# Nine weight transfers in place of six, and a new written order, in a linear-attention and mixer kernel

## The chip, the cores and the metric

The kernel runs on one core of a Trainium2 chip. The metric is device time in microseconds (us): the median of several runs of the whole kernel. Beside these runs stands one profiled execution, from which all durations of single instructions come. The engines have short names in the profile: PE is TensorE (matmuls; PEld its weight loads), DVE is VectorE, ACT is ScalarE, POOL is GpSimd and SP is SyncE, which here only issues transfers. DMA stands for the 16 engines that move data between the main memory (HBM) and the on-chip memory (SBUF). PSUM is the small memory into which PE writes.

## The reference

Inputs r, k and v have the shape (4, 8, 768, 48): four batches, eight heads, 768 steps, 48 channels. The first half is a linear attention with a decaying state for each head, the second half an MLP mixer over its result.

```python
for t in range(S):
    kt, vt, rt = (k[:, :, t], v[:, :, t], r[:, :, t])
    cur = np.einsum('bhd,bhe->bhde', u[None] * kt, vt)
    y[:, :, t] = np.einsum('bhd,bhde->bhe', rt, state + cur)
    state = w[None, :, :, None] * state + np.einsum('bhd,bhe->bhde', kt, vt)
...
xt = x.transpose(0, 2, 1)
h = np.maximum(xt @ w_tok1, 0.0) @ w_tok2
u = x + h.transpose(0, 2, 1)
h2 = np.maximum(u @ w_ch1, 0.0) @ w_ch2
return (u + h2).astype(np.float32)
```

Here x is y with the heads side by side, (4, 768, 384). The token weights are 768 x 256 and 256 x 768, the up weight w_ch1 is 384 x 1536 and the down weight w_ch2 is 1536 x 384.

## The kernel before, in words

**Units.** The attention is done in 24 units: four batches of six chunks of 128 steps (unit u is chunk u % 6 of batch u // 6). A unit loads k, r and v (three transfers of 192 KB, issued by SP). It scales k and r by powers of the decay (kp and rp, L658 and L661; each may run on POOL or DVE, both write the tile kpr), and casts v (vb, ACT). Units 0 to 13 transpose kp and rp on PE (trk, trr into the PSUM tile tr_ps) and copy them back by ACT, either as one copy (rk, L696) or in two halves (rkk and rkr, L700, for the units in `rk_two`); units 14 to 23 transpose by DMA (L684). PE then forms the scores (at, two PSUM tiles), which a causal mask turns into AT0 and AT1 on DVE (L727). For the units in `raw`, AT1 goes another way: ACT copies the scores to SBUF as bf16 (raw, L736), and DVE masks that copy (ATr, L740). PE multiplies with v (y) and with the state of the chunks before (yS), updates the state (kv on PE, S on DVE or ACT), and DVE adds the term of the current step (yd, on DVE or POOL) while it writes the unit's rows of x (L824, tile x_b).

**Mixer.** Once a batch's six units are done: hid (L831) multiplies x with w_tok1 into two PSUM tiles (h_ps), hr applies the relu, and w_tok2 brings it back to tokens. For the first half of batch 0 this is done directly in the transposed layout (ux, ub, uTm, L876 to L892, which write uT); the other halves go by bk, us, tu and uT (tiles hT_ps, u_sb, t_ps). Then z (L899) multiplies uT with w_ch1 in 12 column groups j of 128 for each group sg of three chunks (three matmuls each, 72 for a batch), zr applies the relu (ACT or DVE), and h (L910) multiplies with w_ch2, three column groups at a time (q = 0 to 3). os adds u and a transfer stores the result.

**Order.** Nothing of the order is written by hand. The class `Plan` (L45) holds a list of steps, each with the engines it may use and their assumed times, what it must come after, whether it takes one of four PSUM banks, and a rank. `run` (L72) plays time forward and always starts the open step with the lowest rank whose engine is free; attention has its unit's number as rank, the token half of batch b's mixer (hid to uT) about 6 b + 6.5, its z and h about 1000 + b, so that z and h fill what attention leaves. `graph` (L168) builds the steps, and the instructions are issued on each engine in the order of the plan. An engine's own instructions always run in that order; the semaphores between engines are set by the tile framework from what reads and writes what.

**Weights.** POOL issues the weight transfers (L645), because these convert from float32 to bf16 on the way. There are six: w_tok1, w_tok2, w_ch1 in two halves of 768 columns, and w_ch2 in two halves of rows. `wafter` in the table `CFG` (L436) gives each a step after which it is put into POOL's queue. In the trace they are the transfers to the tiles wtok (two) and wch (four). The load of k of unit 6 is held until the y of unit 5 (`hold`, L456). `fill` puts a few idle matmuls into PE's gaps ahead of the first z.

Of the kernel before, what the change touches and what calls it, by code (L numbers as in the profile page):

```python
# [24 lines left out]
C = S // T  # L25
# [9 lines left out]
class Step:  # L35
    def __init__(self, name, ways, after, take, give, rank, emit):
        self.name, self.ways, self.take, self.give, self.rank, self.emit = name, ways, take, give, rank, emit
        self.after = [a for a in after if a is not None]
        self.then, self.left, self.ready = [], len(self.after), 0.0
        self.engine = self.start = self.end = self.seen = self.sends = None  # L40
        for a in self.after:
            a.then.append(self)


class Plan:  # L45
# [26 lines left out]
    def run(self):  # L72
# [5 lines left out]
        while todo:  # L78
# [4 lines left out]
            while again:  # L83
                again = False
                for s in sorted(open_, key=lambda s: (s.rank, s.ready)):
                    if s.ready > now or (s.take and min(banks) > now):
                        continue
                    if s.sends is not None and len(sent) >= self.in_flight:
                        old = sent[-self.in_flight]
                        if old.seen is None or old.seen > now:  # L90
                            if old.seen is not None:
                                heapq.heappush(times, old.seen)
                            continue
                    way = min(s.ways, key=lambda w: max(now, free.get(w[0], 0.0)) + w[2] + (w[4] if len(w) > 4 else 0.0))
                    eng, busy, seen = way[:3]
# [72 lines left out]
def graph(do, cfg):  # L168
# [24 lines left out]

    loads, weights, fetched, gates, u_row = {}, {}, [], {}, None
    for n, (kind, i) in enumerate(cfg["transfers"]):
        if kind == "b":
            fetched.append(p.add("i:ub", [("SP", cfg.get("sp", 0.65), 0.65)], fetched[-1:], rank=-1000 + n, emit=do("ubc")))
            u_row = p.transfer("x:ub", fetched[-1], 0.63, 1.8, 0.0)
        elif kind != "w":
# [5 lines left out]
        else:  # L205
            weights[i] = n
    wx, wi = {}, {}

    def weight(i, after):
        wi[i] = s = p.add(f"i:w{i}", [("POOL", 0.9, cfg.get("wseen", 1.0), True)], after, rank=-50, emit=do("weight", i))  # L210
        took = cfg.get("wtime", (3.0, 2.6, 3.1, 7.7, 3.1) if 5 not in cfg["wafter"] else (3.0, 2.6, 3.1, 3.9, 3.1, 3.9))[i]
        wx[i] = p.transfer(f"x:w{i}", s, took, took + 1.0, -1.0)

    for i in cfg["wafter"]:
        weight(i, [])
    xs, S_prev, at_free, y_free, kv_read, yS_prev = {}, None, [], None, None, None
    kv_first, bank_read, scored = None, [], {}
    for u in range(NU):
# [19 lines left out]
        if u in turned:  # L238
            s = p.add(f"i:t{u}", [("SP", 1.35, 1.4)], [kp, rp], rank=-2000, emit=do("turn_unit", u))
            rk = p.transfer(f"x:t{u}", s, 1.56, 2.2, 0.0)  # L240
        else:
            trk = p.add(f"trk{u}", [("PE", 0.235 * f, 0.235 * f + 0.2)], [kp], take=True, rank=r, emit=do("trk", u))
            trr = p.add(f"trr{u}", [("PE", 0.235 * f, 0.235 * f + 0.2)], [rp, trk], rank=r - 0.5, emit=do("trr", u))
            if u == 0:
                p.wait(wu, [trr])
            if u in cfg.get("rk_two", ()):
                ways = [("ACT", 0.48, 0.65)] + ([("DVE", 0.38, 0.53, False, cfg["rk_dve"])] if "rk_dve" in cfg else [])
                rkk = p.add(f"rkk{u}", ways, [trk], rank=r, emit=do("rkk", u))
                rk = p.add(f"rkr{u}", ways, [trr], rank=r, emit=do("rkr", u))
            else:  # L250
                rkk = None
                rk = p.add(f"rk{u}", [("ACT", 0.909, 1.08)], [trr], rank=r, emit=do("rk", u))
            reads = [rk, rkk] if rkk else [rk]
            if u in by_pe:
                pr = p.add(f"pr{u}", [("DVE", cfg.get("prt", 0.5), 0.65)], [rk], rank=r - 0.3, emit=do("pr", u))
                reads.append(pr)
            p.add(f"trf{u}", [("-", 0.0, 0.0)], reads, give=[f"trk{u}"], rank=-5000)
# [64 lines left out]
    for b in range(B):  # L322
# [4 lines left out]
        early = old + [xs[b * C + c] for c in range(4)]  # L327
        bank = [p.add(f"hid{b}_bank{i}", [("PE", 0.0, 0.0)], early + [wx[0]], take=True, rank=r) for i in range(2)]
        for c in range(C):
            h = p.add(f"hid{b}_{c}", [("PE", 2 * MM * f, 2 * MM * f + 0.13)], [xs[b * C + c], h] + bank, rank=r, emit=do("hid", b, c))  # L330
        some_direct = [sg for sg in range(2) if (b, sg) in direct]
# [11 lines left out]
        for sg in range(2):  # L343
            if (b, sg) in direct:
                last = C * (b + 1) - 1
                for mm in range(3):
# [10 lines left out]
            for c in range(sg * G, sg * G + G):  # L357
                n = 3 if (b, c) in cfg.get("xpe", ()) else 2
                bk = p.add(f"bk{b}_{c}", [("PE", n * MM + 0.01 * (b > 0), n * MM + 0.13 + 0.01 * (b > 0))], hr + [wx[1]], take=True, rank=r + 0.01 * c, emit=do("bk", b, c))
                us = p.add(f"us{b}_{c}", [ACT1, DVEP] if n == 3 else [DVEP], [bk], give=[f"bk{b}_{c}"], rank=r, emit=do("us", b, c))  # L360
# [9 lines left out]
        for sg in range(2):  # L370
            zr = []
            for j in range(NJ):
                old = downs[2 * b + sg - 3] if 2 * b + sg >= 3 else []
                z = p.add(f"z{b}_{sg}_{j}", [("PE", 3 * MM, 3 * MM + 0.13)], old + uT[3 * sg:3 * sg + 3] + [wx[2] if j < NJ // 2 else wx[4]], take=True, rank=m + 0.1 * sg + 0.001 * j, emit=do("z", b, sg, j))
                ways = [ACT1, DVEP + (False, 0.3)] if b in cfg.get("zr_dve", range(B)) else [ACT1]
                zr.append(p.add(f"zr{b}_{sg}_{j}", ways, [z], give=[f"z{b}_{sg}_{j}"], rank=o, emit=do("zr", b, sg, j)))
            downs.append([])
            for si in range(3):
# [3 lines left out]
                for part in range(parts):  # L382
                    h, n, mm = None, f"{b}_{c}" + "ab"[part] * (parts > 1), MM / parts + (0.005 if parts > 1 else 0.0)
                    for q in range(4):
                        x = 3 * mm + (own if q == 0 else 0.0)
                        h = p.add(f"h{n}_{q}", [("PE", x, x + 0.13)], zr[3 * q:3 * q + 3] + [wx[3] if q < 2 else wx.get(5, wx[3]), h], take=(q == 0), rank=m + 0.1 * sg + 0.05 + 0.01 * si + 0.001 * part - (0.02 if q else 0), emit=do("h", b, c, q, part, parts))
                    ways = [ACT1, DVEP] if (b, sg) in direct else [DVEP]
# [8 lines left out]
    last = None  # L396
    for i, name in cfg["wafter"].items():
        p.wait(wi[i], [last] + [next(s for s in p.steps if s.name == name)])
        last = wi[i]
    for s in p.steps:  # L400
# [32 lines left out]
    + [('b', 0)]  # L433
    + [("u", u) for u in range(14, 24)]
    + [('w', 0), ('w', 1), ('w', 2), ('w', 4), ('w', 3), ('w', 5)],
# [30 lines left out]
def kernel(  # L466
# [529 lines left out]
```

## Time and profile before

| what | us |
| --- | --- |
| median of 3 runs | 165.49 |
| lowest and highest run | 165.25, 165.77 |
| span of the profiled execution | 166.5 |
| mean granted clock of PE in it | 0.990 |
| DVE, ACT and POOL busy in it | 106.8, 87.2, 65.3 |
| first z matmul starts | 30.92 |
| first matmul of the last batch's z after attention is over | 139.72 |
| last h matmul ends | 163.2 |

Times in the profile count from the first instruction of the span. The profiled execution's span is 1.0 us over the median of the timed runs. A group line of the profile gives engine, operation, the tile written and the tiles read, the shape, the count, then the busy time of all in us and the mean of one in ns, then the idle time of the engine just ahead of them and what ended it. A timeline line gives the start in us, the length, engine, operation, tiles and count, and in brackets the idle time before it. The line L512 is that of a helper that records each operation, so the tiles tell the steps apart.

### The profile page before, as it was taken

The numbers are of one execution on the slowest core, as the hardware profiler recorded it, in microseconds if no ns is written. First come the engines' busy times: TensorE is split into PE (matmuls) and PEld (weight loads), VectorE is DVE, ScalarE is ACT, GpSimd is POOL, SyncE is SP. The second block draws the span as 40 slices with busy tenths as digits, with TensorE's granted clock in tenths as the row PEclk, the third lists the DMA queues.
The fourth block names the chain that finished last, engine by engine and source line by source line (L and its number), as shares of the span: only waits on it lengthen the run. The fifth ranks groups of instructions, "written<-read, shape, count | busy, mean of one in ns | idle before, by whom it ended". The sixth has DMA issues, their size and how long they took to land.

```text
span 166.5 us, 3791 instructions
## 1 busy us (share of the span) xinstructions
PE 156.8 (94%) x1462; PEld 100.6 (60%) x1464; DVE 106.8 (64%) x219; ACT 87.2 (52%) x182; POOL 65.3 (39%) x80
## 2 busy tenths in 40 slices
PE   6797999599999999999999999999999999999991
PEld 1377764356677666666666665666656655665671
DVE  5189996300459989899989889977885582021031
ACT  3996743279198636579804452069154502904900
POOL 7839970000009647386785857103840000000000
PEclk9999999789999999999999999999999999999999
DMA  5999999999699899999999994999990028012012
GB/s 100 215 213 210 159 187 176 188 184 168 131 208 287 158 192 216 217 230 182 198 192 169 230 158 106 188 235 222 171 240 6 4 50 218 16 51 94 0 47 94
DMA packets 97427, 26.26 MB, mean 158 GB/s; under 512 B 90753, under 2 KB 97410, under 8 KB 97410
## 3 DMA queue, kind: packets, MB, share of 16 engines
q1 hardware_dynamic: 93920, 22.88, 67.2%
q0 software_dynamic: 3488, 3.15, 12.3%
q8 instruction: 11, 0.18, 0.5%
q14 instruction: 6, 0.05, 0.1%
q10 hardware_dynamic: 2, 0.00, 0.0%
HBM read 20.65 MB, written 4.72 MB: 152 GB/s over the span
## 4 chain that ended last, share of the span: by engine, by line
PE 79%; DMA 8%; POOL 5%; ACT 3%; issue 2%; DVE 1%; SPq 1%; POOLq 0%
PE h_ps L512 31%; PE z_ps L512 29%; DMA wch<-in_moe_w_ch_dram 6%; PE y_ps L512 4%; PE at_ps L512 4%; PE hT_ps L512 3%; PE tr_ps L512 3%; POOL kpr L512 3%; PE kv_ps L512 2%; DMA ld_v<-in_v_dram 2%; PE t_ps L512 1%; ACT rk L512 1%; POOL wtok L512 1%; SPq L512 1%; POOL yd L512 0%
## 5 line engine op out<-in xcount | busy, mean ns | idle before, releaser
L512 ACT ACTIVATE zr<-z_ps 128x384 bf16<-128x384 f32 x94 | 45.5, 492 | 47.5 <-PE z_ps L512 47.3
L512 PE MATMUL z_ps<-uT,wch 128*128 128x384 bf16 x288 | 53.6, 331 | 2.0 <-DMA wch<-in_moe_w_ch_dram 2.0
L512 PE MATMUL h_ps<-wch,zr 128*128 128x384 bf16 (+1 forms) x300 | 52.5, 319 | 0.0
L512 PEld LDWEIGHTS <-wch 128*128 128x128 bf16 x288 | 27.0, 99 | 18.8 <-DMA wch<-in_moe_w_ch_dram 2.4
L512 PEld LDWEIGHTS <-zr 128*128 128x128 bf16 x300 | 27.9, 98 | 15.5 <-issue 0.2
L512 POOL TENSOR_TENSOR yd<-vb,adg 128x384 f32<-128x384 bf16 x18 | 15.5, 860 | 46.5 <-ACT adg L512 27.9
L512 DVE TENSOR_TENSOR AT<-at_ps,mask 128x512 bf16<-128x512 f32 x43 | 27.9, 682 | 0.7 <-PE at_ps L512 0.6
L512 DVE TENSOR_TENSOR osb<-u_sb,h_ps 128x384 f32<-128x384 bf16 (+1 forms) x22 | 11.7, 533 | 23.4 <-PE h_ps L512 23.3
L512 POOL TENSOR_TENSOR kpr<-ld_r,wp 128x384 bf16<-128x384 f32 x16 | 16.6, 1036 | 5.3 <-ACT wp L512 2.8
L512 ACT COPY rk<-tr_ps 128x512 bf16<-128x512 bf16 (+1 forms) x20 | 15.0, 756 | 4.9 <-PE tr_ps L512 4.5
L512 PEld LDWEIGHTS <-kpr 128*128 128x128 bf16 x192 | 13.7, 107 | 6.0 <-POOL kpr L512 2.6
L512 DVE TENSOR_TENSOR x_b<-y_ps,yd 128x384 bf16<-128x384 f32 x24 | 13.2, 552 | 5.2 <-PE y_ps L512 5.1
L512 POOL TENSOR_TENSOR kpr<-ld_k,wn 128x384 bf16<-128x384 f32 x15 | 15.2, 1011 | 1.8 <-DMA ld_r<-in_r_dram 0.7
L512 PEld LDWEIGHTS <-rk 48*128 48x128 bf16 (+1 forms) x272 | 11.0, 99 | 6.4 <-issue 2.7
L512 ACT CAST vb<-ld_v 128x384 bf16<-128x384 f32 x24 | 12.3, 511 | 4.3 <-POOL kpr L512 3.1
L512 PE MATMUL tr_ps<-ident,kpr 128*128 128x128 bf16 x112 | 12.1, 245 | 2.4 <-ACT rk L512 1.4
L512 DVE TENSOR_TENSOR S<-kv_ps,bm 128x384 bf16<-128x384 f32 x13 | 7.2, 551 | 6.0 <-PE kv_ps L512 5.8
L512 DVE TENSOR_TENSOR u_sb<-x_b,hT_ps 128x384 bf16<-128x384 bf16 x21 | 10.4, 546 | 0.9 <-PE hT_ps L512 0.9
L512 PEld LDWEIGHTS <-wtok 128*128 128x128 bf16 x90 | 8.0, 98 | 4.8 <-issue 0.6
L512 PEld LDWEIGHTS <-AT 128*128 128x128 bf16 x192 | 8.4, 98 | 3.4 <-DVE AT L512 0.8
L512 PE MATMUL at_ps<-rk 48*128 48x128 bf16 x192 | 10.2, 229 | 0.2 <-ACT rk L512 0.2
L512 PE MATMUL h_ps<-x_b,wtok 128*128 128x384 bf16 x48 | 10.2, 326 | 0.0
(81 smaller groups left out, 145.4 us busy)
## 6 DMA issues: line engine op xcount, KB each, us to landing
ld_k<-in_k_dram SPq DMA_DIRECT2D x24, 192.0 KB, 3.8
ld_r<-in_r_dram SPq DMA_DIRECT2D x24, 192.0 KB, 3.8
ld_v<-in_v_dram SPq DMA_DIRECT2D x24, 192.0 KB, 3.8
out_dram<-osb SPq DMA_DIRECT2D x23, 192.0 KB, 2.6
wch<-in_moe_w_ch_dram POOLq DMA_DIRECT2D x4, 576.0 KB, 14.2
wtok<-in_moe_w_tok_dram POOLq DMA_DIRECT2D x2, 384.0 KB, 6.4
u_bc<-in_u_dram SPq DMA_DIRECT2D x1, 192.0 KB, 5.0
out_dram<-osb SPq DMA_DIRECT2D x2, 96.0 KB, 1.6
```

The costliest lines, as they stand in the source:

```text
L512: ins = tc.keep_in_program_order(f(*args, **kw))
```

## The change

It changes six things.

- The six weight transfers become nine: w_tok1 in two halves of rows, w_tok2 in two halves of columns, w_ch1 in two quarters (column groups 0 to 2 and 3 to 5) and one half, w_ch2 in two halves of rows as before. Each piece has its columns or rows, an assumed time, and the step after which POOL issues it. The first quarter of w_ch1 is issued ahead of the second half of w_tok2.
- Each step that uses a weight now waits in the plan for the pieces it reads alone (`got`).
- `raw` has ten units in place of five: 0, 1, 4, 5, 6, 7, 12, 13, 18, 19 (8 and 11 are no longer in it). `rk_two` has 1, 3, 4, 5, 6, 8 in place of 0, 1, 2, 3, 4, 6.
- A table `rank` shifts the ranks of 122 steps, by up to about 990 either way, and a table `on` pins 76 steps to one engine. Among these are kp0, rp0, rp1, kp2 and S0, S3 on DVE.
- Some assumed times differ (`pe_times`, `prt`, `slack`, the time of a transfer); they act on the order alone.
- `run` skips steps whose only engine is busy before it sorts them, and computes the fullness of the banks once. This does not alter which step is taken.

```diff
+        self.open_on = ways[0][0] if len(ways) == 1 else None
...
-                for s in sorted(open_, key=lambda s: (s.rank, s.ready)):
-                    if s.ready > now or (s.take and min(banks) > now):
+                full = min(banks) > now
+                for s in sorted([s for s in open_ if s.ready <= now and (s.open_on is None or free.get(s.open_on, 0.0) <= now)], key=lambda s: (s.rank, s.ready)):
+                    if s.take and full:
                         continue
...
-    for i in cfg["wafter"]:
-        weight(i, [])
+    for i, (of, lo, hi, took, after) in enumerate(cfg["pieces"]):
+        wi[i] = s = p.add(f"i:w{i}", [("POOL", 0.85, cfg.get("wseen", 1.0), True)], rank=-50 + 0.01 * i, emit=do("weight", i))
+        wx[i] = p.transfer(f"x:w{i}", s, took, took + cfg.get("wland", 1.3), -1.0 + 0.001 * i)
+
+    def got(of, lo, hi):
+        return [wx[i] for i, (o, a, b, _, _) in enumerate(cfg["pieces"]) if o == of and a < hi and b > lo]
...
+        if s.name in cfg.get("on", {}):
+            s.ways = [w for w in s.ways if w[0] == cfg["on"][s.name]]
+            s.open_on = s.ways[0][0] if len(s.ways) == 1 else None
...
-    wafter={0: 'x:r4', 1: 'x:r4', 2: 'rp5', 4: 'kp5', 3: 'rp5', 5: 'rp5'},
-    slack={'v5': 3.0},
+    pieces=[
+        ('t1', 0, 3, 1.45, 'kp4'),
+        ('t1', 3, 6, 1.45, 'rp4'),
+        ('t2', 0, 3, 1.25, 'x:r5'),
+        ('c1', 0, 3, 1.9, 'x:r5'),
+        ('t2', 3, 6, 1.25, 'x:r5'),
+        ('c1', 3, 6, 1.9, 'x:k5'),
+        ('c1', 6, 12, 3.3, 'x:v5'),
+        ('c2', 0, 6, 4.0, 'rp5'),
+        ('c2', 6, 12, 4.0, 'rp4')],
+    slack={'v5': 1.6},
...
-    raw=(0, 1, 5, 8, 11),
-    rk_two=(0, 1, 2, 3, 4, 6),
+    raw=(0, 1, 4, 5, 6, 7, 12, 13, 18, 19),
+    rk_two=(1, 3, 4, 5, 6, 8),
...
-    pe_times=((0.33, 0.243, 0.185), (0.33, 0.243, 0.185)),
+    pe_times=((0.42, 0.21, 0.175), (0.42, 0.21, 0.175)),
...
-    late={'kp2': -0.6},
+    late={},
...
+    on={
+        'S0': 'DVE', 'S3': 'DVE', 'adg7': 'DVE', 'adg8': 'DVE', 'adg9': 'ACT', 'hr2_0': 'DVE', 'hr2_1': 'DVE',
+        'kp0': 'DVE', 'kp12': 'DVE', 'kp13': 'POOL', 'kp16': 'DVE', 'kp17': 'DVE', 'kp19': 'POOL', 'kp2': 'DVE',
+        'kp22': 'DVE', 'kp8': 'DVE', 'kp9': 'POOL', 'ku19': 'POOL', 'ku20': 'DVE', 'ku22': 'POOL', 'rku14': 'DVE',
+        'rku15': 'DVE', 'rku17': 'DVE', 'rku19': 'DVE', 'rp0': 'DVE', 'rp1': 'DVE', 'rp11': 'POOL', 'rp13': 'POOL',
+        'rp14': 'DVE', 'rp15': 'DVE', 'rp19': 'DVE', 'rp21': 'POOL', 'rp6': 'POOL', 'uT0_3': 'DVE', 'uT0_4': 'ACT',
+        'uT1_1': 'ACT', 'uT1_2': 'ACT', 'uT1_3': 'DVE', 'yd14': 'DVE', 'yd15': 'DVE', 'yd16': 'DVE', 'yd17': 'DVE',
+        'yd19': 'DVE', 'yd20': 'DVE', 'yd8': 'DVE', 'zr0_0_1': 'DVE', 'zr0_0_10': 'DVE', 'zr0_0_2': 'DVE',
...
+        'zr1_0_3': 'DVE', 'zr1_0_4': 'DVE', 'zr1_0_6': 'DVE', 'zr1_1_0': 'DVE', 'zr1_1_10': 'DVE', 'zr1_1_4': 'DVE',
...
     def weight(eng, i):
-        t, src = [(wtok1, moe_w_tok1), (wtok2, moe_w_tok2), (wch1, moe_w_ch1), (wch2, moe_w_ch2), (wch1, moe_w_ch1), (wch2, moe_w_ch2)][i]
-        cols = {2: slice(0, dch // 2), 4: slice(dch // 2, dch)}.get(i, slice(None))
-        rows = {3: slice(0, NJ // 2), 5: slice(NJ // 2, NJ)}.get(i, slice(None)) if 5 in CFG["wafter"] else slice(None)
+        of, lo, hi = CFG["pieces"][i][:3]
+        t, src = {"t1": (wtok1, moe_w_tok1), "t2": (wtok2, moe_w_tok2), "c1": (wch1, moe_w_ch1), "c2": (wch2, moe_w_ch2)}[of]
+        rows, cols = (slice(lo, hi), slice(None)) if of in ("t1", "c2") else (slice(None), slice(lo * 128, hi * 128))
         pool.dma_start(t[:, rows, cols], src.rearrange("(c p) k -> p c k", p=128)[:, rows, cols])
```

More of the change, by code (lines that the diff above doesn't have):

```diff
@@ L93, in run @@
                             continue
-                    way = min(s.ways, key=lambda w: max(now, free.get(w[0], 0.0)) + w[2] + (w[4] if len(w) > 4 else 0.0))
+                    way = s.ways[0] if len(s.ways) == 1 else min(
+                        s.ways, key=lambda w: max(now, free.get(w[0], 0.0)) + w[2] + (w[4] if len(w) > 4 else 0.0))
                     eng, busy, seen = way[:3]
@@ L192, in graph @@
     wgm = p.add("wGm", [("POOL", 1.1, 1.2, True), ("DVE", 0.47, 0.62, True)], [gd], rank=1.5, emit=do("wGm"))
-    loads, weights, fetched, gates, u_row = {}, {}, [], {}, None
+    loads, fetched, gates, u_row = {}, [], {}, None
     for n, (kind, i) in enumerate(cfg["transfers"]):
@@ L254, in graph @@
             if u in by_pe:
-                pr = p.add(f"pr{u}", [("DVE", cfg.get("prt", 0.5), 0.65)], [rk], rank=r - 0.3, emit=do("pr", u))
+                pr = p.add(f"pr{u}", [("DVE", cfg.get("prt", 0.36), 0.65)], [rk], rank=r - 0.3, emit=do("pr", u))
                 reads.append(pr)
@@ L327, in graph @@
         early = old + [xs[b * C + c] for c in range(4)]
-        bank = [p.add(f"hid{b}_bank{i}", [("PE", 0.0, 0.0)], early + [wx[0]], take=True, rank=r) for i in range(2)]
+        bank = [p.add(f"hid{b}_bank{i}", [("PE", 0.0, 0.0)], early + got("t1", 0, 1), take=True, rank=r) for i in range(2)]
         for c in range(C):
-            h = p.add(f"hid{b}_{c}", [("PE", 2 * MM * f, 2 * MM * f + 0.13)], [xs[b * C + c], h] + bank, rank=r, emit=do("hid", b, c))
+            h = p.add(f"hid{b}_{c}", [("PE", 2 * MM * f, 2 * MM * f + 0.13)], [xs[b * C + c], h] + bank + got("t1", c, c + 1), rank=r, emit=do("hid", b, c))
         some_direct = [sg for sg in range(2) if (b, sg) in direct]
@@ L358, in graph @@
                 n = 3 if (b, c) in cfg.get("xpe", ()) else 2
-                bk = p.add(f"bk{b}_{c}", [("PE", n * MM + 0.01 * (b > 0), n * MM + 0.13 + 0.01 * (b > 0))], hr + [wx[1]], take=True, rank=r + 0.01 * c, emit=do("bk", b, c))
+                bk = p.add(f"bk{b}_{c}", [("PE", n * MM + 0.01 * (b > 0), n * MM + 0.13 + 0.01 * (b > 0))], hr + got("t2", c, c + 1), take=True, rank=r + 0.01 * c, emit=do("bk", b, c))
                 us = p.add(f"us{b}_{c}", [ACT1, DVEP] if n == 3 else [DVEP], [bk], give=[f"bk{b}_{c}"], rank=r, emit=do("us", b, c))
@@ L385, in graph @@
                         x = 3 * mm + (own if q == 0 else 0.0)
-                        h = p.add(f"h{n}_{q}", [("PE", x, x + 0.13)], zr[3 * q:3 * q + 3] + [wx[3] if q < 2 else wx.get(5, wx[3]), h], take=(q == 0), rank=m + 0.1 * sg + 0.05 + 0.01 * si + 0.001 * part - (0.02 if q else 0), emit=do("h", b, c, q, part, parts))
+                        h = p.add(f"h{n}_{q}", [("PE", x, x + 0.13)], zr[3 * q:3 * q + 3] + got("c2", 3 * q, 3 * q + 3) + [h], take=(q == 0), rank=m + 0.1 * sg + 0.05 + 0.01 * si + 0.001 * part - (0.02 if q else 0), emit=do("h", b, c, q, part, parts))
                     ways = [ACT1, DVEP] if (b, sg) in direct else [DVEP]
@@ L396, in graph @@
     last = None
-    for i, name in cfg["wafter"].items():
-        p.wait(wi[i], [last] + [next(s for s in p.steps if s.name == name)])
+    for i, piece in enumerate(cfg["pieces"]):
+        p.wait(wi[i], [last] + [next(s for s in p.steps if s.name == piece[4])])
         last = wi[i]
@@ L433 @@
     + [('b', 0)]
-    + [("u", u) for u in range(14, 24)]
-    + [('w', 0), ('w', 1), ('w', 2), ('w', 4), ('w', 3), ('w', 5)],
-    wafter={0: 'x:r4', 1: 'x:r4', 2: 'rp5', 4: 'kp5', 3: 'rp5', 5: 'rp5'},
-    slack={'v5': 3.0},
+    + [("u", u) for u in range(14, 24)],
+    pieces=[
[9 more added lines that the diff above has]
+    slack={'v5': 1.6},
     pe_turn=(0, 1),
@@ L460 @@
     fill_from=16.5,
+    x_act=(),
+    rank={
[22 rows of a table added]
+    on={
[12 rows of a table added]
     fill=(0.24, 0.09, 0.13),
```

15 lines of the change are left out of this document (4 added, 11 removed), and 26 rows, old and new, of tables (on, rank).

## Prediction, made before the result was known

> **What bounds the kernel now.** I read the page first, for the share of each engine and the slices.
>
> ```profile
> span 166.5 us, 3791 instructions
> ...
> PE 156.8 (94%) x1462; PEld 100.6 (60%) x1464; DVE 106.8 (64%) x219; ACT 87.2 (52%) x182; POOL 65.3 (39%) x80
> ...
> PE   6797999599999999999999999999999999999991
> ```
>
> TensorE (PE) is full from the ninth slice (33 us) to the end; the holes lie ahead of it. So I cut the time into windows (columns: width, busy time and instructions of PE, PEld, DVE, ACT, POOL, then granted clock, DMA share, GB/s; in the second fence PE alone).
>
> ```profile
> 20.00:25.00 5.00, 4.67 (x73) 3.29 (x73) 5.00 (x12) 2.21 (x4) 4.11 (x5) 1.00 1.19 187
> ...
> 30.00:35.00 5.00, 4.08 (x21) 2.50 (x22) 0.72 (x2) 1.68 (x4) 0.00 (x0) 0.66 1.25 186
> ...
> 60.00:80.00 20.00, 19.49 (x237) 13.14 (x234) 18.39 (x38) 14.02 (x29) 12.64 (x14) 1.00 1.02 210
> ```
>
> ```profile
> 29.00:30.00 1.00, 0.00 (x0) 1.00 1.12 196
> ...
> 33.00:34.00 1.00, 1.00 (x5) 0.50 1.27 186
> ```
>
> Around 30 us PE stands still, and right after that it runs at half clock. Over 30 to 35 the granted clock is 0.66 on average, so 5 x 0.34 = 1.7 us of work is lost, in 3.4 us at 0.50. After that only 60 to 80 leaves idle time worth naming (0.5 us). PE's waits and the timeline name the cause.
>
> ```profile
> PE z_ps L512 <- DMA wch<-in_moe_w_ch_dram: 2.0, 1, 2.0
> ```
>
> ```profile
> 25.34 0.56 DVE L512 TENSOR_TENSOR x_b<-y_ps,yd 128x384 bf16<-128x384 f32 x1 [0.16 <-PE y_ps L512]
> ...
> 27.96 0.56 DVE L512 CAST uT<-ut_ps 128x384 bf16<-128x384 f32 x1 [0.76 <-PE ut_ps L512]
> 28.43 1.47 DVE L512 TENSOR_TENSOR u_sb<-x_b,hT_ps 128x384 bf16<-128x384 bf16 x3
> ...
> 30.92 0.85 PE L512 MATMUL z_ps<-uT,wch 128*128 128x384 bf16 x3 [2.02 <-DMA wch<-in_moe_w_ch_dram]
> ```
>
> Batch 0 of attention ends at 25.9 (x_b of unit 5). The transposed activations uT of the first group are ready at 28.5, but the first half of the up weight is there only at 30.9. The chain of waits (start, length, what) and POOL's queue say why.
>
> ```profile
> 20.86 10.02 DMA wch<-in_moe_w_ch_dram
> ...
> 31.77 1.05 PE t_ps L512 x9
> ...
> 111.79 3.42 PE z_ps L512 x21
> ```
>
> ```profile
> 18.15 0.78 POOL L512 DMA_DIRECT2D wtok<-in_moe_w_tok_dram  x1
> ...
> 20.86 3.26 POOL L512 DMA_DIRECT2D wch<-in_moe_w_ch_dram  x4
> ```
>
> The DMA engines are full (shares 1.19 and 1.25 above), and the weights pass in the order of issue. **The bound is DMA until 31 us, then PE.**
>
> **The change, part by part.** All sums are differences on the profiled execution, whose span of 166.5 is 1.0 over the median of 165.49; I take them off the median.
>
> *Nine pieces.* What lies ahead of the first up projection decides, so I need packet times. A packet is one row of one partition: 768 columns of 2 bytes make the large packets of 27.7 to 29.0 (wch1 alone on its queue, first row), 384 columns the small ones of 33 to 37 (wch2, second row).
>
> ```profile
> q0 software_dynamic: 173, 0.26, 110.7%
> ```
>
> ```profile
> q0 software_dynamic: 779, 0.59, 93.8%
> ```
>
> 1.107 x 16 x 1.3 us / 173 = 133 ns for a large packet; 0.938 x 16 x 4 / 779 = 77 ns for a small one. Before, wtok2 (256 large) and half of wch1 (384 large) take 640 x 133 / 16 = 5.3 us. After, half of wtok2 (256 small) and a quarter of wch1 (384 small) take 640 x 77 / 16 = 3.1 us. The first quarter lands at 30.9 - 2.2 = 28.7, against uT at 28.5: 1.8 of the 2.0 us go. If the slowest DMA engine is late whatever is queued, nothing goes (lower bound 0); the upper bound is the 2.0.
>
> The next quarter follows the other half of wtok2, 3.1 us later (31.8). Until then PE has three z of the first group and three of the second, 18 matmuls at 0.163 (3.42 / 21) = 2.9 us, and nine transposes (0.5 to 1.0; the row was at half clock): 3.4 or more for 3.1 us. But its order must wait for u_sb (29.9), so I charge 0.5 (bounds 0 and 1.5). The rest of wch1 needs 384 x 133 / 16 = 3.2 us more (35.0), under the next six z (2.9 us). With no gap of 2 us the clock stays up: 1.7 us gained (bounds 0 and 1.7).
>
> The row for the clock is the 0.50 above, right after a gap of 2.0 us. The Trainium skill, "TensorE: Matmul & The Clock Gate", section "HAM oscillation", sees the danger in idle gaps over about 3.4 us; by that rule this gap would have cost no clock, and the sum would lack the 1.7. The trace disagrees, so that outcome gets no chance of its own.
>
> Small packets cost DMA time: for wtok2 512 x 77 against 256 x 133, for half of wch1 768 x 77 against 384 x 133, together (39.4 - 34.0 + 59.1 - 51.1) / 16 = 0.8 us. Three more issues cost POOL 3 x 0.82 = 2.5 us (3.26 / 4 each); what queues behind them are kp and rp of unit 5. Their cover: kp0, rp0 and rp1 leave POOL (3 x 1.0 us, next rows).
>
> *Order and engines of batch 0.*
>
> ```profile
> L512 DVE TENSOR_TENSOR AT<-at_ps,mask 128x512 bf16<-128x512 f32 x43 | 27.9, 682 | 0.7 <-PE at_ps L512 0.6
> ...
> L512 POOL TENSOR_TENSOR kpr<-ld_k,wn 128x384 bf16<-128x384 f32 x15 | 15.2, 1011 | 1.8 <-DMA ld_r<-in_r_dram 0.7 <-PE z_ps L512 0.5 <-issue 0.5
> ...
> L512 DVE TENSOR_TENSOR kpr<-ld_r,wp 128x384 bf16<-128x384 f32 x8 | 4.7, 593 | 5.1 <-DMA ld_r<-in_r_dram 5.1
> ...
> L512 DVE TENSOR_TENSOR AT<-raw,mask_b 128x512 bf16<-128x512 bf16 x5 | 2.5, 504 | 0.0
> ```
>
> kp0 and rp0 take 2.0 us on POOL and 1.2 on VectorE (DVE), which is free that early: 0.8 sooner. But DVE is full later (5.00 of 5 from 20 to 25). The second mask of unit 4, now by way of a ScalarE copy, takes 0.18 off it (682 - 504), and S3, now on DVE, adds about the 0.55 of any such operation. Net 0, bounds 1.0 either way: the 0.8 and the 0.2, or S3 and one more product of 0.6 paid. In all ten second masks instead of five go by copies: 5 x 0.18 = 0.9 us off DVE, with ScalarE half idle (52%); all but unit 4's lies under PE's full stage.
>
> *What is late next.* With 1.8 + 1.7 - 0.5 = 3.0 us in hand PE finishes batch 0's mixer sooner, and then batch 1's attention must feed it. Its loads (the landing is that of the row at 54.78, v of unit 11):
>
> ```profile
> 42.50 0.56 DVE L512 TENSOR_TENSOR kpr<-ld_r,wp 128x384 bf16<-128x384 f32 x1 [4.85 <-DMA ld_r<-in_r_dram]
> ...
> 67.46 0.55 DVE L512 TENSOR_TENSOR x_b<-y_ps,yd 128x384 bf16<-128x384 f32 x1
> ```
>
> ```profile
> 45.84 0.61 PE L512 MATMUL tr_ps<-ident,kpr 128*128 128x128 bf16 x8
> ```
>
> ```profile
> 54.78 2.30 SPq L512 DMA_DIRECT2D ld_v<-in_v_dram  x1
> ```
>
> ```profile
> DMA to landing us min/median/max: 4.8/4.8/4.8
> ```
>
> The last load of unit 11 lands at 54.8 + 4.8 = 59.6 and its x_b ends at 68.0: 8.4 us. From rows like those above, a unit's own chain is an estimated 5.0 (product 1.0, two masks 1.4, x_b 0.55, and about 2 for transposes, copy, scores and y). So 3.4 us can be drawn in, less the 0.8 of DMA: 2.6 of the 3.0 survive. Sum: **165.5 - 2.6 = 162.9**.
>
> **Rivals.** *A, the loads pace batch 1.* Unit 6 starts after a load that is there at 42.5, and SP sends in the same order. If only its transposes move (45.8 to about 45.2), PE empties sooner and then waits: 0.6 gained, 164.9. For it: a DMA share of 1.02 in 60 to 80. Against: the 8.4 us.
>
> *B, DVE becomes the bound of batch 2.*
>
> ```profile
> 75.00:105.00 30.00, 30.00 (x280) 18.66 (x278) 28.01 (x54) 14.78 (x33) 20.77 (x21) 1.00 0.94 176
> ```
>
> ```profile
> L512 POOL TENSOR_TENSOR yd<-vb,adg 128x384 f32<-128x384 bf16 x18 | 15.5, 860 | 46.5 <-ACT adg L512 27.9 <-ACT vb L512 11.1 <-DVE adg L512 7.4
> ...
> L512 DVE TENSOR_SCALAR zr<-z_ps 128x384 bf16<-128x384 f32 x2 | 1.1, 558 | 0.2 <-PE z_ps L512 0.2
> ```
>
> ```profile
> uT<-u_sb SPq DMA_TRANSPOSE x4, 3.3
> ```
>
> ```profile
> 103.10 1.29 SPq L512 DMA_TRANSPOSE uT<-u_sb  x1
> ```
>
> ```profile
> 108.19 0.65 PE L512 MATMUL z_ps<-uT,wch 128*128 128x384 bf16 x3
> ```
>
> DVE has 2.0 us free of 30. The new pins put six zr of batch 1 and yd of units 14 to 17, 19 and 20 there: 12 x 0.56 = 6.7 us. That is over by 4.7, unless other products go to POOL, which has 9 us left. Batch 2's uT is issued at 103.1, takes 3.3 and is used at 108.2: 1.8 us of slack. B decides once the overload passes 1.8 us plus what was gained: 4.7 - 1.8 - (0 to 2.6) = 0.3 to 2.9 slower, middle 167.1.
>
> ```profile
> 65.15 1.00 POOL L512 TENSOR_TENSOR kpr<-ld_r,wp 128x384 bf16<-128x384 f32 x1
> ```
>
> ```profile
> 65.68 0.75 DVE L512 TENSOR_TENSOR AT<-raw,mask_b 128x512 bf16<-128x512 bf16 x1
> ```
>
> A copied mask that runs beside a POOL product takes 0.75, more than the 0.68 of the direct one. The Trainium skill, "SBUF — State Buffer", section "Who interferes with whom", has a DVE operation with two SBUF inputs and a GpSimd operation that reads SBUF hold a shared pair of ports in turn; by that rule each of the five more copied masks could cost DVE 0.07 instead of saving 0.18. The row agrees.
>
> *C, the change does not do what it says:* the slowest DMA engine is late with the first quarter too, or a later quarter is 1.5 us late and the clock falls all the same; 165.5.
>
> *D, the whole opening moves:* the upper bounds together, 2.0 + 1.7 + 1.0 = 4.7; 160.8.
>
> **How the numbers follow.** Forecast 0.50 (its own range 161.4 to 164.4, from the bounds of 1.5 for the quarters and 1.0 for the opening), A 0.14, B 0.20, C 0.06, D 0.10. A measurement of this kernel tells about 0.3%, 0.5 us. Faster: 0.50 + 0.10 + 0.12 of A = 0.72; same: C and the rest of A, 0.08; slower 0.20. The range runs from just below D to the middle of B, 160.3 to 167.0.
>
> **What would show it.** Right: PE's wait on wch under 0.5 us, a granted clock of 1.00 from 30 to 35, batch 0's 72 z matmuls done by 42, x_b of unit 11 done near 65.4. A: x_b of unit 11 still near 68, with PE idle before it. B: DVE without gaps from 75 to 105 and z of batch 2 after 108.2. C: a wait of 1.5 us or more on wch and a clock under 0.7. The forecast would be wrong if PE's written order stalls on one of the later quarters for over 1.5 us.

## The result, and the profile after

The changed kernel takes 173.62 us (median of 4 runs, 173.25 to 173.85), the kernel before 165.45 (165.25 to 165.77) beside it: a ratio of 1.0507, 95% interval 1.0479 to 1.0536. It is 8.2 us slower; 162.9 was forecast. Ratios here compare undisturbed runs alone, so one can differ a little from the quotient of the medians. The first fence is the page of the changed kernel; the second its windows (columns as in the prediction), the third PE's waits.

```profile
span 171.7 us, 3774 instructions
...
PE 160.2 (93%) x1462; PEld 101.8 (59%) x1464; DVE 123.4 (72%) x261; ACT 73.7 (43%) x151; POOL 62.9 (37%) x76
...
PE   6979999469999999999999899999999999999992
```

```profile
20.00:25.00 5.00, 4.78 (x66) 3.46 (x65) 3.79 (x9) 3.34 (x7) 4.98 (x7) 1.00 0.76 81
...
30.00:35.00 5.00, 2.07 (x13) 1.03 (x11) 0.57 (x2) 0.49 (x1) 0.00 (x0) 0.91 1.10 206
35.00:40.00 5.00, 4.35 (x31) 2.95 (x32) 3.84 (x9) 1.39 (x3) 2.65 (x3) 0.50 1.15 195
40.00:45.00 5.00, 5.00 (x30) 2.85 (x28) 3.54 (x8) 3.12 (x8) 0.00 (x0) 0.91 1.26 187
...
75.00:105.00 30.00, 29.19 (x284) 18.23 (x283) 29.72 (x59) 14.77 (x32) 15.50 (x15) 1.00 0.90 177
```

```profile
PE tr_ps L559 <- DVE zr L559: 3.4, 1, 3.4
```

PE again stands still once around 30 us, but longer: 2.07 of 5 us busy from 30 to 35. The granted clock of 0.91, 0.50 and 0.91 over three windows is 0.9 + 5.0 + 0.9 = 6.8 us at 0.50, from 34.1 to 40.9. PE stands still until 35.51 (below), so 5.4 us of them fall on work, and 2.7 us of work are lost. No row of PE's waits names wch any more. The timeline shows what PE stands behind.

```profile
29.69 1.24 PE L559 MATMUL z_ps<-uT,wch 128*128 128x384 bf16 x6
...
31.42 0.65 PE L559 MATMUL z_ps<-uT,wch 128*128 128x384 bf16 x3
...
34.43 0.56 DVE L559 TENSOR_TENSOR kpr<-ld_k,wn 128x384 bf16<-128x384 f32 x1 [4.52 <-DMA ld_k<-in_k_dram]
34.91 0.55 DVE L559 TENSOR_SCALAR zr<-z_ps 128x384 bf16<-128x384 f32 x1
35.04 0.10 PEld L559 LDWEIGHTS <-kpr 128*128 128x128 bf16 x1 [3.36 <-DVE kpr L559]
35.19 0.99 POOL L559 TENSOR_TENSOR kpr<-ld_r,wp 128x384 bf16<-128x384 f32 x1 [9.97 <-DMA ld_r<-in_r_dram]
35.37 1.01 DVE L559 TENSOR_TENSOR u_sb<-x_b,hT_ps 128x384 bf16<-128x384 bf16 x2
35.51 1.33 PE L559 MATMUL tr_ps<-ident,kpr 128*128 128x128 bf16 x8 [3.44 <-DVE zr L559]
...
36.13 0.88 POOL L559 DMA_DIRECT2D wch<-in_moe_w_ch_dram  x1
```

The first quarter of the up weight is there in time: z starts at 29.69 without waiting. But DVE has kp6, the product on k of unit 6, in front of the relu zr and of u_sb. Its load was requested after seven weight pieces, DVE waits 4.52 us for it, and with DVE all that is queued behind. PE's own order has the transpose of kp6 next, ahead of the rest of batch 0's mixer: its weight load waits 3.36 us for kp6, then the transpose waits for the relu behind kp6 as well. PE gets its next work at 35.51. POOL does the same with rp6 (9.97 us), and the last two weight pieces stand behind it: they are issued at 36.13, where before all were issued by 24.1.

Before, kp6 stood behind everything that batch 0's mixer needs. The repeated run of the unchanged kernel shows it, and something else (fences: page, windows, timeline).

```profile
span 163.5 us, 3793 instructions
...
PE 155.6 (95%) x1464; PEld 99.9 (61%) x1464; DVE 106.7 (65%) x219; ACT 87.0 (53%) x182; POOL 65.3 (40%) x80
```

```profile
25.00:30.00 5.00, 5.00 (x47) 2.90 (x44) 3.49 (x9) 1.57 (x5) 0.00 (x0) 1.00 1.14 194
30.00:35.00 5.00, 4.88 (x34) 2.97 (x34) 1.01 (x3) 4.53 (x10) 0.00 (x0) 1.00 1.26 185
```

```profile
25.82 0.56 DVE L512 TENSOR_TENSOR x_b<-y_ps,yd 128x384 bf16<-128x384 f32 x1 [0.16 <-PE y_ps L512]
...
28.92 1.47 DVE L512 TENSOR_TENSOR u_sb<-x_b,hT_ps 128x384 bf16<-128x384 bf16 x3
...
36.47 0.56 DVE L512 TENSOR_TENSOR kpr<-ld_k,wn 128x384 bf16<-128x384 f32 x1 [5.29 <-DMA ld_k<-in_k_dram]
...
64.45 0.54 DVE L512 TENSOR_TENSOR x_b<-y_ps,yd 128x384 bf16<-128x384 f32 x1
```

DVE waits even longer for k (5.29 us), with nothing behind it that PE needs. And here PE has neither the 2.0 us wait on wch nor the half clock: the span is 163.5, where the execution shown in the prediction had 166.5. (In the repeated run only PE's weight load for the first z waits for wch, 0.19 us.)

The sum, against this typical execution, up to x_b of unit 11 (rows of after below):

```profile
26.84 0.56 DVE L559 TENSOR_TENSOR x_b<-y_ps,yd 128x384 bf16<-128x384 f32 x1 [0.46 <-PE y_ps L559]
...
72.48 0.56 DVE L559 TENSOR_TENSOR x_b<-y_ps,yd 128x384 bf16<-128x384 f32 x1 [0.20 <-PE y_ps L559]
```

Unit 5's x_b starts 1.0 later (26.84 against 25.82); the stall is 3.4; the half clock costs 2.7: together 7.1. x_b of unit 11 is 8.0 later (72.48 against 64.45), the end 8.2 (171.7 against 163.5). Most is lost before 41 us; the 0.9 between 7.1 and 8.0 was not located. By the pages, PE is busy 4.6 us longer (160.2 against 155.6) and idle 3.6 us longer (11.5 against 7.9).

### The profile page after: what moved, and what is told of

Read it like the earlier page. It is cut to its first block, busy times and chain, and to the rows that moved or that the text cites. A ratio compares the mean times of both kernels' runs of the same rounds, so it can differ in the third digit from the quotient of the medians.

```text
span 171.7 us, 3774 instructions
## 1 busy us (share of the span) xinstructions
PE 160.2 (93%) x1462; PEld 101.8 (59%) x1464; DVE 123.4 (72%) x261; ACT 73.7 (43%) x151; POOL 62.9 (37%) x76
## 4 chain that ended last, share of the span: by engine, by line
PE 73%; DMA 9%; DVE 8%; SPq 3%; POOL 2%; issue 1%; ACT 1%; POOLq 0%
PE h_ps L559 28%; PE z_ps L559 25%; PE y_ps L559 5%; DMA ld_r<-in_r_dram 5%; PE at_ps L559 4%; PE hT_ps L559 3%; PE tr_ps L559 3%; SPq L559 3%; PE kv_ps L559 3%; DMA ld_v<-in_v_dram 3%; DMA ld_k<-in_k_dram 2%; DVE AT L559 2%; POOL kpr L559 2%; PE t_ps L559 1%; DVE kpr L559 1%
## 5 line engine op out<-in xcount | busy, mean ns | idle before, releaser
L559 ACT ACTIVATE zr<-z_ps 128x384 bf16<-128x384 f32 x65 | 31.6, 492 | 38.5 <-PE z_ps L559 38.2
L559 DVE TENSOR_TENSOR AT<-at_ps,mask 128x512 bf16<-128x512 f32 x38 | 24.9, 680 | 0.1
L559 DVE TENSOR_SCALAR zr<-z_ps 128x384 bf16<-128x384 f32 x31 | 16.9, 553 | 9.9 <-PE z_ps L559 8.6
L559 POOL TENSOR_TENSOR yd<-vb,adg 128x384 f32<-128x384 bf16 x11 | 9.4, 854 | 34.6 <-DVE adg L559 28.8
L559 PEld LDWEIGHTS <-kpr 128*128 128x128 bf16 x192 | 14.3, 112 | 10.7 <-DVE kpr L559 4.4
L559 PE MATMUL tr_ps<-ident,kpr 128*128 128x128 bf16 x112 | 13.1, 264 | 5.1 <-DVE zr L559 3.4
L559 PEld LDWEIGHTS <-rk 48*128 48x128 bf16 (+1 forms) x272 | 11.5, 103 | 7.2 <-issue 2.8
L559 DVE TENSOR_TENSOR u_sb<-x_b,hT_ps 128x384 bf16<-128x384 bf16 x21 | 10.7, 545 | 2.3 <-PE hT_ps L559 2.2
L559 POOL TENSOR_TENSOR ku<-ld_k,u_bc 128x384 f32<-128x384 f32 x9 | 9.7, 1073 | 4.9 <-DMA ld_k<-in_k_dram 2.6
L559 PE MATMUL at_ps<-rk 48*128 48x128 bf16 x192 | 10.8, 240 | 0.2 <-ACT rk L559 0.2
L559 ACT CAST raw<-at_ps 128x512 bf16<-128x512 f32 x10 | 5.9, 586 | 12.0 <-PE at_ps L559 12.0
```

Source lines behind the costliest of these rows:

```text
L559: ins = tc.keep_in_program_order(f(*args, **kw))
```

## The experiments

**Theory 1**: the written order. The plan believes that k and r of unit 6 land early, puts their products ahead of batch 0's mixer on in-order engines, and on the chip these wait behind the weights. **Theory 2**: VectorE, which has 16.6 us more to do, becomes the bound. **Rival P**: nine pieces are slow in themselves. Ratios are to the kernel before on the same chip, with 95% intervals.

### Was there anything to gain?

`before_again`, no edit.

> The kernel before, unchanged, with the span and clock of each execution. If the profiled execution on which the prediction was built (span 166.5) is typical, the spans are 166 to 167 again, PE waits 2 us for wch and the clock falls to one half after it. If it was an unlucky one, the spans lie near 163.4 (the changed kernel's time of 173.76 stands 2.06 over its span of 171.7, and 165.4 less 2.06 is 163.4), and the wait or the half clock, 3.7 us together, is missing from the trace.

165.53 us, ratio 1.0015 (0.9993 to 1.0036). The ten timed executions have spans of 163.0 to 164.8 and clocks of 0.997 to 1.000; the time is about 1.7 us above the span of the same execution. So the execution that the prediction read lay some 3 us over the typical one, in which PE does not wait for wch. Why that one execution was slower is not known.

`b_first_quarter`, the gain's carrier alone:

```diff
+        if i == 2:
+            pool.dma_start(t[:, :, 0:384], src.rearrange("(c p) k -> p c k", p=128)[:, :, 0:384])
+            cols = slice(384, 768)
```

> The kernel before in its own written order; only the first half of the up weight is cut into two quarters, issued one behind the other at the place of the half (one more issue of about 0.75 us on POOL, behind kp5 and rp5). It is the part of the change on which the prediction's gain rested, alone. Theory 1 (in the repeated run of before PE does not wait for the up weight: z starts at 29.22, right behind its transposes, and 0.64 us are idle from 26 us to the end): nothing to gain, 165.0 to 165.6. The prediction's own theory (2.0 us of wait and 1.7 of half clock to be gained): 162 to 163.5.

164.83 us, ratio 0.9972 (0.9953 to 0.9991): about 0.5 us faster than before, a little more than theory 1 expected, and the fastest kernel of this study. The quarter is worth 0.5 us, not 3.0. Where the 0.5 comes from its trace does not show: the first z starts 0.4 us earlier (28.82 against 29.22), but so does what stands ahead of it (ut_ps at 27.52 against 27.92).

`b_nine_in_place`, before's order with its weights cut into the nine:

```diff
+        nine = {0: [("t1", 0, 3), ("t1", 3, 6)], 1: [("t2", 0, 3), ("c1", 0, 3), ("t2", 3, 6)], 2: [("c1", 3, 6)],
+                4: [("c1", 6, 12)], 3: [("c2", 0, 6)], 5: [("c2", 6, 12)]}
```

> The kernel before in its own written order on every engine; only the six weight transfers are cut into the nine pieces (the first quarter of the up weight ahead of the second half of w_tok2), issued at the places in POOL's queue where the six stood. Theory 1 (the pieces hurt only through the order that the plan made of them): the smaller packets make the last weight and unit 6's loads up to 0.8 us later, against 2.9 us between the landing of r of unit 6 (39.95) and its transposes (42.83): 165.0 to 166.0. Rival P (the pieces themselves are slow on the DMA engines): the transposes of unit 6 come later than 43.5 and the time is over 167.

166.34 us, ratio 1.0079 (1.0047 to 1.0110), a little above what theory 1 expected. POOL (first fence: the repeated before; second: this kernel) shows why.

```profile
20.07 1.00 POOL L512 TENSOR_TENSOR kpr<-ld_r,wp 128x384 bf16<-128x384 f32 x1
21.01 3.25 POOL L512 DMA_DIRECT2D wch<-in_moe_w_ch_dram  x4
```

```profile
22.22 1.00 POOL L512 TENSOR_TENSOR kpr<-ld_r,wp 128x384 bf16<-128x384 f32 x1
23.16 3.25 POOL L512 DMA_DIRECT2D wch<-in_moe_w_ch_dram  x4
...
27.26 0.56 DVE L512 TENSOR_TENSOR x_b<-y_ps,yd 128x384 bf16<-128x384 f32 x1 [0.22 <-PE y_ps L512]
```

Three more issues ahead of rp5 put it 2.15 us back, and unit 5's x_b comes 1.44 later (27.26 against 25.82). The pieces cost by their issues, about 1.3 us; rival P's 167 isn't reached, though its other sign, transposes of unit 6 later than 43.5, is there (44.27), 1.44 later like x_b.

### The product in front

`b_kp6_first`, before with one step moved:

```diff
+    six = [s for s in steps if s.name in ("kp6",)]
+    steps = [s for s in steps if s not in six]
+    at = next(n for n, s in enumerate(steps) if s.name == "us0_3")
+    steps[at:at] = six
```

> The kernel before with one step moved: kp6 (the product on k of unit 6) is written on VectorE ahead of the first group's u_sb instead of behind its uT; six weights, no other edit. In the repeated run of before k of unit 6 landed at 36.4 and VectorE then waited 5.3 us for it, with nothing queued behind. Theory 1 (an in-order engine is blocked by a product whose load is behind the weights): u_sb moves from 28.9 to 37.0, PE stalls after its first three z for some 7.6 us, and a gap of this length is followed by 3.4 to 6.8 us at half clock (1.7 to 3.4 lost): 165.4 + 7.6 + 1.7 to 3.4 = 174.7 to 176.4. Theory 2 (VectorE's added load costs the time): VectorE has the same work, so 165.4, at most 166.

175.22 us, ratio 1.0629 (1.0584 to 1.0674), inside theory 1's range. PE's waits:

```profile
PE t_ps L512 <- DVE u_sb L512: 8.1, 1, 8.1
```

```profile
36.81 0.56 DVE L512 TENSOR_TENSOR kpr<-ld_k,wn 128x384 bf16<-128x384 f32 x1 [8.26 <-DMA ld_k<-in_k_dram]
37.29 1.48 DVE L512 TENSOR_TENSOR u_sb<-x_b,hT_ps 128x384 bf16<-128x384 bf16 x3
```

In this trace the granted clock was 0.50 from 34.85 to 41.65, and PE had work again from 37.89: 3.8 us at half clock with work, 1.9 lost. 8.1 + 1.9 = 10.0 of the 10.2 measured. One product in the wrong place costs 10 us. That is the mechanism by itself.

`b_pieces`: before with the nine pieces and the change's waits on them, planned anew; masks, pins and ranks as before.

> The kernel before with the nine pieces alone; masks, pins, ranks and assumed times stay as before, and the plan is made anew. Theory 1 (a load of unit 6 that the plan believes landed at 28 to 29 heads the in-order queues of DVE and POOL): DVE has kp6 and rp6 ahead of u_sb of batch 0, r of unit 6 lands near 42, so PE stalls for several us after the first z and the time is 170 or more. Theory 2 (the pins overload DVE): DVE's work is that of before, 123 minus 17 us, so the time is within 2 us of before, 163 to 167.

183.08 us, ratio 1.1054 (1.0981 to 1.1127), as theory 1 expected (170 or more). PE's largest wait:

```profile
PE tr_ps L523 <- DVE kpr L523: 11.1, 2, 9.9
```

`b_pieces_k6_known_late`: the same, and the plan is told when unit 6's loads land.

```diff
-    slack={'v5': 3.0},
+    slack={'v5': 3.0, 'k6': 9.0, 'r6': 13.0},
```

> The kernel before with the nine pieces planned as pieces (183.1 by itself), where the plan is told that k and r of unit 6 land 9 and 13 us later than it works out (36.5 and 42.1, as on the chip, in place of 27.5 and 29.1); the whole order is planned anew. The plan's own end is 163.6 against 160.9 for before. Theory 1 (the order made from the wrong landing is the cause): PE's stalls on unit 6 go, and the time follows the plan: 166.5 to 169. Rival P (pieces in themselves): over 173.

167.87 us, ratio 1.0162 (1.0122 to 1.0202): 15 of the 17.8 us come back by two numbers that only tell the plan a landing. The mistake can be followed in the code. The plan spaces the chained issues 1.75 us apart (`wseen`); small pieces of 1.25 to 1.9 us leave gaps in its DMA, into which k and r of unit 6 slip, and played forward it starts kp6 at 27.5. With six pieces of 2.6 to 5.2 us it has no gaps and starts kp6 at 41.2. On the chip POOL issues one piece each 0.75 to 0.82 us, and the queue is solid. The plan of the changed kernel, played forward, makes the same mistake: kp6 at 28.7 on DVE and rp6 at 29.2 on POOL, where the chip started them at 34.43 and 35.19. The changed kernel planned anew with the true landings was not run.

`b_pieces_unit6_later`: `b_pieces` with unit 6's steps moved by hand ahead of kp7.

> The kernel before with the nine pieces planned as pieces (183.1 by itself), and the steps of unit 6 (kp6, rp6, transposes, copies, scores, masks) moved behind, to stand ahead of kp7. Theory 1: PE's two stalls on kp6 and rp6 (9.9 and about 2, and the half clock of 10.2 us behind them, 5.1 lost) go; what is left is the weights' end, some 1 to 4 us later than in before: 166 to 169. Rival P (pieces are slow in themselves): over 173.

173.21 us, ratio 1.0505 (1.0455 to 1.0555): 10 us come back, fewer than expected. The expectation counted 5.1 us lost in 10.2 us at half clock; in the trace of `b_pieces` these run from 30.85 to 41.05 and PE stands still until 37.97, so about 1.5 were lost. And all later units still stand in the order made for the wrong landing; the plan made anew, above, is 5 us faster.

### The stall taken out of the changed kernel

`a_unit6_later`: kp6 to pr6, eleven steps, put ahead of h0_5_0 in one block.

> The changed kernel with its own written order, except that the eleven steps of unit 6 from the products to the masks are issued later, ahead of h0_5_0. Theory 1: PE's wait of 3.4 us near 32 and the half clock of 6.8 us (3.4 us lost) go, and POOL issues the last two pieces near 26 instead of 36: 5 to 7 us gained, 166.5 to 168.5. Theory 2: DVE stays full from 60 to 120, so at most 1.5 us is gained, 172 or more.

172.04 us, ratio 1.0398 (1.0356 to 1.0439): 1.6 us back of an expected 5 to 7. As a number that is theory 2's 172; the trace decides. Its windows, and PE's waits from 40 us on:

```profile
20.00:22.00 2.00, 1.69 (x23) 1.30 (x24) 0.82 (x3) 1.03 (x2) 1.98 (x4) 1.00 0.23 20
...
45.00:50.00 5.00, 2.49 (x18) 1.37 (x19) 2.29 (x5) 1.66 (x3) 0.20 (x1) 0.85 1.08 209
50.00:55.00 5.00, 5.00 (x53) 3.08 (x52) 1.47 (x5) 2.78 (x6) 0.68 (x1) 0.81 0.95 199
```

```profile
PE at_ps L559 <- ACT rk L559: 1.2, 1, 1.2
PE h_ps L559 <- DVE pr L559: 1.1, 1, 1.1
PE tr_ps L559 <- POOL kpr L559: 0.3, 1, 0.3
```

The stall came back 13 us later, as 2.6 us of waits on unit 6 with 5 x (0.15 + 0.19) = 1.7 lost at half clock. Some of that my block made itself: PE had nothing between the unit's transposes and its scores. The DMA share of 0.23 from 20 to 22 us shows a second cause: the pieces stand behind kp5 and rp5 in POOL's queue, so that DMA runs dry, and the last weight and r of unit 6 land some 4 us later than before.

`a_unit6_later_early_issue`: the same block, and three issues moved up in POOL's queue.

```diff
+    for one, ahead in (("i:w1", "kp5"), ("i:w2", "kp5"), ("i:w3", "rp5")):
```

> The changed kernel with unit 6's steps moved ahead of h0_5_0 (172.0 by itself) and, besides, three weight issues moved up in POOL's queue: the second half of w_tok1 and the first of w_tok2 ahead of kp5, the first quarter of the up weight ahead of rp5. In the run without this the DMA engines had a share of 0.23 from 20 to 22 us, the last weight landed at 43.9 and r of unit 6 at 44.1, after which PE waited 2.6 us and ran 3.4 us at half clock. Theory 1 with late issues as its second half: the weights end 2 to 2.5 us earlier, the waits on unit 6 fall under 0.7 and the half clock behind them goes: 168 to 169.5. Theory 2 (VectorE's load): no change, 171 to 172.

171.67 us, ratio 1.0402 (1.0349 to 1.0455): no gain that can be told. The weights did end 3.4 us earlier, but unit 5's x_b came 1.2 us later, and the two waits of 1.2 and 1.1 stayed. Theory 1 missed, and theory 2's 171 to 172 holds as a number. In the opening kp5 starts 0.35 us later on its load (19.62 against 19.27 in `a_unit6_later`), PE waits 2.1 us for it (0.9 there), the granted clock is 0.50 from 21 to 26, and v of unit 5 lands 3.5 us later (24.05 against 20.5). That DMA time spent on weights early is taken from unit 5 fits this; which of the four makes unit 5 late was not separated.

`a_unit6_spread`: scores and masks of unit 6 three h quarters behind its transposes.

> The changed kernel with kp6, rp6, transposes, copies and pr of unit 6 moved ahead of h0_5_0 as before (172.0 with all of unit 6 there in one block), but its scores and masks three h quarters later, ahead of h0_1_2, so that PE has 1.5 us of work between. In the block PE waited 1.16 and 1.10 us for the unit's own copies and then ran 3.4 us at half clock. Theory 1: these 2.3 us and the 1.7 lost at half clock go: 167.5 to 169. What is left over before would be the opening (x_b of unit 5 at 28.0 against 26.4) and weights that end 4 us later. Theory 2 (VectorE's load): 171 to 172.

171.12 us, ratio 1.0353 (1.0315 to 1.0391); theory 1 missed as well, theory 2's range holds. POOL still waits 15.7 us for r, to 42.64, and PE 1.0 us for rp6, 1.6 for pr.

`a_unit6_last`: the unit ahead of h0_2_2, 2 us further back.

> The changed kernel with unit 6's products, transposes, copies and pr moved still further behind, ahead of h0_2_2 (2.0 us of h quarters later than in the run where they stood ahead of h0_5_0, 171.1), and its scores and masks ahead of the transposes of unit 7. In that earlier run r of unit 6 landed at 42.5, PE waited 1.0 us for rp6 and 1.6 us for pr, and then ran 3.4 us at half clock. If these waits are what is left of the stall: no wait on unit 6 over 1.2 us, no half clock after 40 us, 167.5 to 169. If VectorE's load is what is left: 170.5 to 171.5.

170.43 us, ratio 1.0279 (1.0212 to 1.0346): 167.5 to 169 missed again, and just below VectorE's range. Its trace (of the longest of its four executions) has waits of 1.5, 0.7 and 0.7 on unit 6 and a clock of 0.50 from 50 to 52. By their ratios the block, the spread and this one give back 1.8, 2.5 and 3.8 us of the 8.4 (0.0507 x 165.4). Each time the unit still waits for its own loads and copies, so none of these runs has the stall simply gone, and none by itself tells it from VectorE's load.

### VectorE's load

`a_relu_on_act`: the 22 relus of batches 1 to 3 that are pinned to DVE run on ACT.

```diff
+    for s in steps:
+        if s.name[:3] in ("zr1", "zr2", "zr3") and CFG["on"].get(s.name) == "DVE":
+            s.engine = "ACT"
```

> The changed kernel with its own written order, except that the 22 relus of batches 1 to 3 that are pinned to DVE run on ACT. That takes 22 x 0.47 = 10 us of DVE's 123. Theory 2: DVE is no longer full from 60 to 120 and 3 us or more are gained, 170.5 or less. Theory 1: the stall at 32 to 41 stays and nothing much is gained, 172.5 to 174.

172.81 us, ratio 1.0450 (1.0414 to 1.0487): 0.8 us back, as theory 1 expected, so DVE's load by itself is not what lost most of the 8.2.

`b_relu_on_dve`: the reverse in the kernel before, the same 22 from ACT to DVE.

> The kernel before in its own order, with the 22 relus of batches 1 to 3 that the change pins to VectorE put there from ScalarE; nothing else. VectorE has 28.0 us of 30 busy from 75 to 105, and nine of these relus (0.56 each) fall near there. Rival B of the prediction (VectorE becomes the bound): 166.5 to 169. If VectorE's load costs nothing as long as PE is fed: 165 to 166.

167.13 us, ratio 1.0104 (1.0047 to 1.0160): 1.8 us lost by them alone. Theory 2 is right for a part; its place (windows, and PE's waits from 60 us on):

```profile
75.00:85.00 10.00, 10.00 (x81) 6.14 (x80) 9.90 (x19) 3.64 (x8) 7.96 (x8) 1.00 1.00 189
85.00:95.00 10.00, 9.12 (x100) 5.60 (x98) 9.45 (x18) 3.62 (x8) 6.25 (x8) 1.00 1.05 197
```

```profile
PE y_ps L512 <- DVE x_b L512: 0.8, 1, 0.8
```

`a_unit6_spread_relu` and `a_unit6_last_relu`: the two moves of unit 6, with the 22 relus on ACT besides.

> The same, and besides the 22 relus zr of batches 1 to 3 that are pinned to VectorE run on ScalarE (some 12 us off VectorE, which is full from 75 to 125 us). Theory 1: PE never waits for VectorE there, so within 1 us of the kernel without this. Theory 2 (a full VectorE costs time once PE is no longer late): 3 us or more faster than the kernel without this.

> The same with the 22 relus of batches 1 to 3 on ScalarE. If the stall's return is all: within 1 us of the kernel without this, 167 to 169. If both count: 1.5 to 2.5 us faster than it, 165.5 to 167.5, so that nearly the whole loss of 8.2 us is accounted for.

168.95 us, ratio 1.0224 (1.0194 to 1.0254), and 169.27, ratio 1.0235 (1.0185 to 1.0284). For the first, 2.2 us from the relus; theory 1 had expected under 1, theory 2 3 or more, so neither holds alone. For the second, 1.2 us by the medians and 0.7 by the ratios, whose intervals overlap, and 3.9 us over before remain, where 165.5 to 167.5 was expected. Both changes together give back 4.7 and 4.5 of the 8.4. The second's trace holds waits of 0.7 and 0.6 on unit 6, and an opening that is 1.1 late (the first z starts at 29.25 against 29.22, but the six hT products that stood ahead of it, 1.14 in all, are still to come): some 2.4. The last 1.5 stay open.

## Why the prediction was wrong

**The gain.** The step "1.8 of the 2.0 us go", with "1.7 us gained" from the clock, failed first. Both were read from an execution that was 3 us slower than the runs it was set beside. The prediction put its span "1.0 over the median", but the timed value holds some 1.7 us more than the span, so span against span it was some 3 over; a span longer than the longest timed run (166.5 against 165.77) should have been the warning. In the typical execution PE was not waiting for the weight, and the quarter alone is worth 0.5.

**The later quarters.** "I charge 0.5 (bounds 0 and 1.5)" is the step that gave the wrong sign. No quarter was late: no z waited. PE stalled on kp6 and on what stood behind it on DVE, for 3.4 us, and lost 2.7 more at half clock, where the step charged 0.5. The step looked at PE's z and at the weights; it did not ask what the new order puts in front on DVE, POOL and PE itself, and when the load of that lands. The prediction's last sentence named a stall of over 1.5 us, for the wrong transfer. That this mechanism suffices is shown by `b_kp6_first`, that it comes from the planned landing, in the kernel before with the nine pieces, by `b_pieces_k6_known_late`. For the changed kernel itself the stall and its plan are read from trace and code; no run takes it out cleanly.

**Nine issues on POOL.** "Their cover: kp0, rp0 and rp1 leave POOL" failed: on POOL these had ended by 9.1 us, the pieces are issued from 16.5 on, and what is free early covers nothing there. `b_nine_in_place` measures 1.4 us on unit 5. In the changed kernel itself the same queue hurt the other way round: rp5 is hardly late, the pieces are.

**Batch 0's order.** "Net 0, bounds 1.0 either way" came out at its upper bound, 1.0. What in it costs the 1.0 was not isolated.

**Masks.** Ten at 486 ns in place of 680: 0.19 each, as costed (0.18). No run tried them alone, so whether any of it reaches the end is not shown.

**Rivals.** A did not get to decide: PE was late itself. B was real and smaller than the cause: 1.8 us alone, inside its 0.3 to 2.9, and 0.7 (not clear of noise) to 2.2 in the changed kernel (0.8 by `a_relu_on_act`). Its sign is there in the windows of after: from 75 to 105 DVE is busy 29.72 of 30 us and PE 29.19, where before PE had no gap. C had the nearest shape (a late wait, a fallen clock) but not the place. What happened was on no list.

## What to carry to other kernels

Before a wait in one profiled execution is counted as a gain, set its span beside spans, or look for the wait in a second execution. Where an order is planned and engines run in order, take for every instruction that moves in front of the critical one the landing of its data in the trace, not in the plan; a load requested behind large weights holds up all that stands behind its first reader. And compare the plan's own constants with the trace (issues 1.75 us apart against 0.75 to 0.82).

## What the runs showed of the hardware

**Loads behind weights.** In the repeated before, SP issued k of unit 6 at 25.81, and its product started at 36.47, 10.7 us later; the median of k's loads is 3.8 on the page of after. A load of 192 KB is 1024 rows of 192 bytes, 64 for each of 16 DMA engines. If they take turns with weight packets of 133 ns (the prediction's figure), one row for one packet, they need 64 x 133 = 8.5 us, an estimate; that leaves 2.2 of the 10.7 for all the rest. The Trainium skill, "DMA: Bandwidth & Descriptors", section "Queues, rings and completion order", says that each engine goes round the queues that have work, one packet (of several descriptors) at a time. The trace agrees with the turns: the last weight was issued at 23.4, ahead of k, and landed at 39.7, behind it. It does not show how much goes in one turn. No run here varies the rows of a load.

**The clock.** In the changed kernel the clock fell to 0.50 2.0 us into the wait of 3.4 and stayed there for 6.8; the 2.0 us wait of the prediction was followed by 3.4 us at 0.50, and two waits of 1.2 and 1.1 close together in `a_unit6_later` also by 3.4. Half clock costs only where PE has work: in `b_kp6_first` 3.0 of its 6.8 us fell into the wait. The same transposes (rows of after, then of the repeated before) show that PE was also slow for longer in the changed kernel's opening, though the column of the granted clock has 1.00 there:

```profile
19.76 0.61 PE L559 MATMUL tr_ps<-ident,kpr 128*128 128x128 bf16 x4 [0.30 <-POOL kpr L559]
...
22.21 0.63 PE L559 MATMUL tr_ps<-ident,kpr 128*128 128x128 bf16 x4 [0.22 <-issue]
```

```profile
19.13 0.38 PE L512 MATMUL tr_ps<-ident,kpr 128*128 128x128 bf16 x4
...
21.21 0.40 PE L512 MATMUL tr_ps<-ident,kpr 128*128 128x128 bf16 x4
```

Whether that is what makes unit 5 1.0 us late was not tried.
